# Pinned magnitudes, a norm moved by one attention pair, score banks for the gated layer, and shifted blocks in one fused fp32 kernel

## The chip, the cores and the metric

One Trainium2 chip, and one core of it: the program uses no other. The metric is the device time of one execution in microseconds (us); lower is better. Five engines work beside each other and meet through semaphores: TensorE (PE, with its weight loads as PEld), VectorE (DVE), ScalarE (ACT), GpSimd (POOL) and SyncE (SP), whose queue issues every DMA transfer here.

## The reference

Attention with sigmoid in place of softmax, a gated layer with a root-mean-square norm, and a layer with a product of two projections. Weights come as float64 and are decoded on the chip.

```python
scores = scale * np.matmul(q, k.transpose(0, 1, 3, 2)) - np.log(S)   # q, k, v: (4, 12, 448, 64)
attn = 1.0 / (1.0 + np.exp(-scores))
x = np.matmul(attn, v)                                  # then (1792, 768)
rms = np.sqrt(np.mean(x * x, axis=-1, keepdims=True) + 1e-06)
xn = x / rms * rms_g
g = xn @ w_gate                                         # 768 -> 1536
x = (g * sigmoid(g) * (xn @ w_val)) @ w_out             # 1536 -> 768
h = (x @ w1) * (x @ w2) @ w3                            # 768 -> 1024 -> 1024
out = h @ w_out                                         # 1024 -> 768
```

## The kernel before

The work is done per batch (four batches of 448 tokens). Every matrix operand is split into a high and a low part in fp32r, and each product is three matmuls (`mm3`, L293 to L295). The stages follow each other on PE in this order:

- attention pairs 0 to 11 (batches 0 and 1, two heads to a pair, `visit` L406, one pair to a visit); meanwhile DVE and POOL decode and split the eight tiles o0 to o7 of the second `w_out` (`decode_wo2`) and the first tiles of `w3`;
- the first products w3·w_out (`w3o_group`, L330, results copied out by ACT at L340);
- the first half of the gated layer for batches 0 and 1 (`a_group` L579, for m = 0 to 5; four units to an m, with a further w3·w_out product behind each four), each unit 18 matmuls into one PSUM bank, then a sigmoid (ACT L584) and products (DVE L585, L589);
- attention pairs 12 to 23 (batches 2 and 3), one visit at a time, set between the other half of the gated units and the first `b_group` units by a running sum of costs (L694 to L700);
- the rest of `b_group`; beside it `x_blocks` (L508) makes the right-hand operands of the next stage on DVE and ACT;
- batches 2 and 3 by Strassen-Winograd with seven products instead of eight: the gated layer (`winograd` L521), then `b_units(1)`, then the next layer c for both pairs of batches with `d_units` between and behind.

A weight tile is loaded as float64 (`wd`, L94, two buffers), decoded by `to_float` (L97): the absolute value on ACT (L104) or, for the first six tiles, on DVE (L106), then DVE L109, L110, L118, L121 into `wf`; then split by ACT L128 (or POOL L130) and POOL L131 into `ws` (four buffers). The magnitude `mag` has one buffer. `wo2` tiles (o0 to o7) go the same way with the magnitude on DVE. "Ahead" tiles (`add_ahead`, table `AHEAD_B1`) are `w1`/`w2` tiles decoded early and put into DRAM for the c layer.

`rms_norm` (L440) sums over partitions with one matmul (PE L442, reading `acc`, which POOL L436 adds up) into one of the three banks of `ps_m`, and that bank is read by ACT L446 and DVE L447; then DVE L448 to L453 make r, which `split_x` (`load_x` L466, `split2` L309 to L312) needs. PSUM has three `ps_m` banks, one for attention's output, and four (two tiles of two) for scores, L391 reading the latter with the sigmoid; the third score block uses `ps_m` and L389.

The order on each engine is not the written one: a scheduler of the framework places each instruction by estimated times, and engines run their lists strictly in that order. `tc.keep_in_program_order(i)` pins an instruction behind those written before it. The diff touches `to_float`, `split_to`, `accumulate`, `a_group`, and the main sequence (L646 to L711).

Of the kernel before, what the change touches and what calls it, by code (L numbers as in the profile page):

```python
# [8 lines left out]
F32 = mybir.dt.float32  # L9
F32R = mybir.dt.float32r  # L10
U32 = mybir.dt.uint32
AF = mybir.ActivationFunctionType
# [17 lines left out]
W3_FIRST = 3  # L30


AHEAD_B1 = (1, 1, 1, 1, 0, 0)
AHEAD_B2 = (2, 2, 2, 1, 1, 0)
WH = 3 * P

# [6 lines left out]
def fused_kernel(ctx: ExitStack, tc: tile.TileContext, qkv, wg, wv, wo, w1, w2, w3, wo2, gam, out):  # L43
# [38 lines left out]
    def psm():  # L82
        return ps_m.tile([P, 512], F32, tag="m", bufs=3, name="psm")
# [10 lines left out]
        nc.sync.dma_start(out=d, in_=src.bitcast(U32))  # L94
        return t

    def to_float(raw, w, scalar=True):  # L97

        lo, hi = raw[:, :w, 0], raw[:, :w, 1]
        mag = wp.tile([P, WT], F32, tag="mag", bufs=1, name="mag")[:, :w]  # L100
        f = wp.tile([P, WT], F32, tag="wf", bufs=2, name="wf")
        u = f[:, :w].bitcast(U32)
        if scalar:
            nc.scalar.activation(mag, hi.bitcast(F32), AF.Abs)  # L104
        else:
            nc.vector.tensor_scalar(  # L106
                out=mag.bitcast(U32), in0=hi, scalar1=0x7FFFFFFF, scalar2=None, op0=ALU.bitwise_and
            )
        nc.vector.tensor_scalar(out=mag, in0=mag, scalar1=HI_MIN, scalar2=HI_MAX, op0=ALU.max, op1=ALU.min)  # L109
        nc.vector.tensor_scalar(  # L110
            out=u,
            in0=mag.bitcast(U32),
            scalar1=3,
            scalar2=0x3FFFFFFF,
            op0=ALU.logical_shift_left,
            op1=ALU.bitwise_and,
        )
        nc.vector.scalar_tensor_tensor(  # L118
            out=u, in0=hi, scalar=0xC0000000, in1=u, op0=ALU.bitwise_and, op1=ALU.bitwise_or
        )  # L120
        nc.vector.scalar_tensor_tensor(  # L121
            out=u, in0=lo, scalar=29, in1=u, op0=ALU.logical_shift_right, op1=ALU.bitwise_or
        )
        return f
# [8 lines left out]
    class Weights:  # L133
# [58 lines left out]
        def split_to(self, n):  # L192

            n = min(n, len(self.seq) - 1)
            while self.n_split <= n and len(self.split) < self.BUFS:
                i = self.n_split
                self.load_to(i)
                src, kt, double, keep, use = self.seq[i]
                f = self.raw.pop(i)
                w = WT if kt is None else kt * P  # L200
                if double:
                    f = to_float(f, w, i >= 2 * W3_FIRST)
                    if keep is not None:
                        nc.sync.dma_start(out=keep, in_=f[:, :w].rearrange("p (k c) -> p k c", c=P))
                    self.out -= 1
                self.finish()
                if not use:
                    self.n_split += 1
                    continue
                t = wp.tile([P, 2, WT], F32R, tag="ws", bufs=self.BUFS, name="ws")  # L210
                self.split[i] = [t, 2]
                self.n_split += 1
                if kt is None:
                    for j in range(2):
                        split_weight(t[:, :, j * WH : (j + 1) * WH], next(self.blocks), WH)
                elif double:
                    self.late = (i, t, f, w, i >= 2 * W3_FIRST)
                else:
                    split_weight(t, f, w)
                    self.out -= 1  # L220
# [73 lines left out]
        nc.tensor.matmul(ps, wh, xt[:, 1, :], start=False, stop=False)  # L294
        nc.tensor.matmul(ps, wh, xt[:, 0, :], start=False, stop=last)  # L295

    def accumulate(tiles, xts):
        ps = psm()[:, :S]
        n = len(xts)
        j = 0  # L300
        for t, kt in tiles:
            for kw in range(kt):
                mm3(ps, t, kw, xts[j], j == 0, j == n - 1)
                j += 1
        return ps
# [134 lines left out]
    def rms_norm(b):  # L440
        ps = psm()[:, :S]
        nc.tensor.matmul(ps, ones, acc.pop(b), start=True, stop=True)  # L442
        v = scratch("v")
        r = rms[b] = scr.tile([P, S], F32, tag="r", bufs=2, name="r")
        t = scratch("t")
        nc.scalar.activation(t, ps, AF.Sqrt, bias=eps_b, scale=1.0 / DM)  # L446
        nc.vector.tensor_scalar(out=v, in0=ps, scalar1=1.0 / DM, scalar2=EPS, op0=ALU.mult, op1=ALU.add)  # L447
        nc.vector.reciprocal(r, t)  # L448

        nc.vector.tensor_tensor(out=t, in0=r, in1=r, op=ALU.mult)  # L450
        nc.vector.tensor_tensor(out=t, in0=t, in1=v, op=ALU.mult)
        nc.vector.tensor_scalar(out=t, in0=t, scalar1=-0.5, scalar2=1.5, op0=ALU.mult, op1=ALU.add)
        nc.vector.tensor_tensor(out=r, in0=r, in1=t, op=ALU.mult)  # L453
# [19 lines left out]
    def split_x(b, k):  # L473

        if k < KD:
            ready.append(load_x(b, k))
        if k:
            t = acts["x", b, k - 1] = x_tile("x", b)
            split2(t, ready.pop(0), b == 1)
# [28 lines left out]
    def x_blocks(k):  # L508
        right_blocks(k, load_x(2, k), load_x(3, k), load_x(2, k + 3), load_x(3, k + 3))
# [68 lines left out]

    def a_group(m, b, which):  # L579
        t = W.get(i_a[m][which])  # L580
        ps = accumulate([(t, 6)], [acts["x", b, k] for k in range(KD)])
        if which == 0:
            s = scratch("s")
            nc.scalar.activation(s, ps, AF.Sigmoid)  # L584
            nc.vector.tensor_tensor(out=s, in0=ps, in1=s, op=ALU.mult)  # L585
            half[m, b] = s
        else:
            s = half.pop((m, b))
            nc.vector.tensor_tensor(out=s, in0=ps, in1=s, op=ALU.mult)  # L589
            t = h_tile("hm", m)  # L590
            split2(t, s)
            acts["h", b, m] = t
# [53 lines left out]
    for i in range(NA + 1):  # L646
        visit(i, (0, NA, 2))
        with tc.issue_after(last_raw[0]):
            if i in DECODE:
                decode_wo2(DECODE[i])  # L650
                load_wo2(DECODE[i] + 2)
            if i in W3_AT:
                W.load_to(W3_AT[i] + 1)
                W.split_to(W3_AT[i] - 1)
        if i == HP:
            rms_norm(0)
        if i > HP:
            split_x(0, i - HP - 1)
    split_x(0, KD)


    def w3o_groups(kt):
        for nh in range(2):
            w3o_group(kt, nh)
            W.split_to(i_w3[kt][1] + 2 + nh)
            W.load_to(i_w3[kt][1] + 4 + nh)

    w3o_groups(0)
    rms_norm(1)
    for k in range(KD + 1):  # L670
        if k % 3 == 2:
# [22 lines left out]
    total, spent = sum(u[0] for u in beside), 0.0  # L694
    for j, u in enumerate(beside):
        spent += run(u, int(j >= half_a and j % 2 == 1))
        while visits and NP + 1 - NA - len(visits) < (NP + 1 - NA) * spent / total:
            visit(visits[0], (NA, NP, 1))
            if visits.pop(0) == NA + HP:
                rms_norm(2)  # L700
# [6 lines left out]
    pools["xw"] = pool("xw", "left")  # L707
    for j, u in enumerate(b[6:]):
        run(u, j % 2)
        if j % 2 == 0:  # L710
            x_blocks(j // 2)  # L711


    for m in range(KF1):
# [75 lines left out]
```

## Time and profile before

| | us |
|---|---|
| median of 3 runs | 1122.58 (1122.19 to 1125.78) |
| the profiled execution | 1121.57 |
| its span in the trace | 1119.8 |
| PE busy (share of span) | 1079.6 (96%) |
| DVE busy | 730.1 (65%) |
| ACT busy | 469.0 (42%) |
| POOL busy | 434.6 (39%) |
| mean granted clock of PE | 0.988 |

The span lacks 1.8 us of the execution, and the execution lies 1.0 us below the median. Times in rows count from the start of the span. A bracket at the end of a row, as [2.50 <-POOL acc L436], is the time its engine had nothing to do before it, and what ended that. PEclk is the share of full speed that PE was granted in a stretch: 1.0 is 2.4 GHz, 0.5 is 1.2 GHz.

### The profile page before, as it was taken

What the parts mean: (1) busy time and instruction counts of PE and PEld (TensorE: products, weight loads), DVE (VectorE), ACT (ScalarE), POOL (GpSimd) and SP (SyncE); (2) the same over time, 40 slices, a digit from 0 to 9 for tenths busy, and PEclk for the clock granted to TensorE, in tenths of its full rate; (3) what the DMA queues carried; (4) which work ended last, traced back from release to release, by engine and by line L of the source; (5) the groups of instructions that cost most, each with busy time, mean ns of one, the idle gap of its engine ahead of it and who ended that gap; (6) DMA issues with size and microseconds to landing.
All of it is one profiled execution on the core that took longest, in us unless ns stands there. A gap on an engine that the chain in (4) does not pass through costs nothing. (4 is left out here: it accounts for less than half of the span.)

```text
span 1119.8 us, 14158 instructions
## 1 busy us (share of the span) xinstructions
PE 1079.6 (96%) x5132; PEld 897.4 (80%) x5132; DVE 730.1 (65%) x996; ACT 469.0 (42%) x811; POOL 434.6 (39%) x336
## 2 busy tenths in 40 slices
PE   8996999998999999999999999999999999999998
PEld 3334988996766667699899999889989999999997
DVE  5985975567444645369889988666788726677500
ACT  5762433343455554534444443344433335333221
POOL 2743322333122113223566564223465533565420
PEclk9998999999999999999999999999999999999999
DMA  7733455447354355565111212676421243220131
GB/s 248 258 121 100 132 180 174 147 155 279 133 185 143 133 198 193 189 206 180 66 58 58 75 66 70 219 264 221 144 90 60 82 143 132 74 76 29 44 100 50
DMA packets 60981, 153.23 MB, mean 137 GB/s; under 512 B 5872, under 2 KB 32624, under 8 KB 60912
## 3 DMA queue, kind: packets, MB, share of 16 engines
q1 hardware_dynamic: 60912, 152.33, 40.0%
q8 instruction: 41, 0.67, 0.2%
q14 instruction: 28, 0.23, 0.1%
HBM read 114.95 MB, written 37.36 MB: 136 GB/s over the span
## 5 line engine op out<-in xcount | busy, mean ns | idle before, releaser
L131 POOL TENSOR_TENSOR ws<-wf,ws 128x768 fp32r<-128x768 f32 (+1 forms) x88 | 150.0, 1707 | 382.8 <-ACT ws L128 312.8
L293 PE MATMUL w<-w,ws 128*128 128x448 f32 x588 | 217.4, 370 | 4.4 <-POOL ws L131 2.2
L294 PE MATMUL w<-w,ws 128*128 128x448 f32 x588 | 217.4, 370 | 0.7 <-DVE w L312 0.7
L295 PE MATMUL w<-w,ws 128*128 128x448 f32 x588 | 216.7, 369 | 0.0
L131 POOL TENSOR_TENSOR ws<-wd,ws 128x384 fp32r<-128x384 f32 x112 | 128.4, 1161 | 92.1 <-ACT ws L128 85.3
L131 POOL TENSOR_TENSOR ws<-s,ws 128x384 fp32r<-128x384 f32 x84 | 99.0, 1183 | 79.2 <-ACT ws L128 77.4
L104 ACT ACTIVATE mag<-wd 128x768 f32<-128x768 f32 (+1 forms) x62 | 53.9, 869 | 178.7 <-DMA wd<-in_w 54.6
L293 PEld LDWEIGHTS w<-w,ws 128*128 128x128 f32 x588 | 111.1, 189 | 17.2 <-POOL ws L131 2.6
L294 PEld LDWEIGHTS w<-w,ws 128*128 128x128 f32 x588 | 111.2, 189 | 11.2 <-DVE w L312 1.0
L295 PEld LDWEIGHTS w<-w,ws 128*128 128x128 f32 x588 | 111.3, 189 | 10.6
L293 PE MATMUL psm<-x,ws 128*128 128x448 f32 x288 | 108.7, 377 | 8.0 <-DVE s L585 5.3
L110 DVE TENSOR_SCALAR wf<-mag 128x768 uint32<-128x768 uint32 (+1 forms) x76 | 57.1, 752 | 84.8 <-POOL ws L131 78.0
L293 PE MATMUL psm<-hm,ws 128*128 128x448 f32 x288 | 106.8, 371 | 1.1 <-POOL ws L131 1.1
L294 PE MATMUL psm<-hm,ws 128*128 128x448 f32 x288 | 105.8, 367 | 0.5 <-DVE hm L312 0.5
L294 PE MATMUL psm<-x,ws 128*128 128x448 f32 x288 | 106.1, 369 | 0.0
L295 PE MATMUL psm<-x,ws 128*128 128x448 f32 x288 | 106.1, 368 | 0.0
L295 PE MATMUL psm<-hm,ws 128*128 128x448 f32 x288 | 105.3, 365 | 0.0
L109 DVE TENSOR_SCALAR mag<-mag 128x768 f32<-128x768 f32 (+1 forms) x76 | 49.8, 655 | 51.4 <-ACT mag L104 50.9
L128 ACT ACTIVATE ws<-wf 128x768 fp32r<-128x768 f32 (+1 forms) x82 | 61.3, 750 | 51.2 <-PE psm L295 22.7
L118 DVE SCALAR_TENSOR_TENSOR wf<-wd,wf 128x768 uint32<-128x768 uint32 (+1 forms) x76 | 80.9, 1064 | 2.2
L128 ACT ACTIVATE ws<-wd 128x384 fp32r<-128x384 f32 x112 | 54.5, 514 | 58.3 <-PE w L295 34.5
L121 DVE SCALAR_TENSOR_TENSOR wf<-wd,wf 128x768 uint32<-128x768 uint32 (+1 forms) x76 | 77.3, 1016 | 1.5
(113 smaller groups left out, 1991.7 us busy)
## 6 DMA issues: line engine op xcount, KB each, us to landing
raw<-in_qkv SPq DMA_DIRECT2D x23, 736.0 KB, 4.5
wd<-in_wo SPq DMA_DIRECT2D x20, 768.0 KB, 5.8
wd<-in_w SPq DMA_DIRECT2D x16, 768.0 KB, 5.2
wd<-w SPq DMA_DIRECT2D x32, 384.0 KB, 3.6
wd<-in_wg SPq DMA_DIRECT2D x12, 768.0 KB, 4.7
wd<-in_wv SPq DMA_DIRECT2D x12, 768.0 KB, 4.6
wd<-in_w SPq DMA_DIRECT2D x16, 512.0 KB, 4.4
w<-wf SPq DMA_DIRECT2D x16, 384.0 KB, 2.5
```

The lines of the kernel that those rows point to most:

```text
L104: nc.scalar.activation(mag, hi.bitcast(F32), AF.Abs)
L109: nc.vector.tensor_scalar(out=mag, in0=mag, scalar1=HI_MIN, scalar2=HI_MAX, op0=ALU.max, op1=ALU.min)
L110: nc.vector.tensor_scalar(out=u, in0=mag.bitcast(U32), scalar1=3, scalar2=0x3FFFFFFF, op0=ALU.logical_shift_left, op1=ALU.bitwise_and,)
L118: nc.vector.scalar_tensor_tensor(out=u, in0=hi, scalar=0xC0000000, in1=u, op0=ALU.bitwise_and, op1=ALU.bitwise_or)
L121: nc.vector.scalar_tensor_tensor(out=u, in0=lo, scalar=29, in1=u, op0=ALU.logical_shift_right, op1=ALU.bitwise_or)
L128: nc.scalar.activation(t[:, 0, :w], f[:, :w], AF.Copy)
L131: nc.gpsimd.tensor_tensor(out=t[:, 1, :w], in0=f[:, :w], in1=t[:, 0, :w], op=ALU.subtract)
L293: nc.tensor.matmul(ps, wl, xt[:, 0, :], start=first, stop=False)
L294: nc.tensor.matmul(ps, wh, xt[:, 1, :], start=False, stop=False)
L295: nc.tensor.matmul(ps, wh, xt[:, 0, :], start=False, stop=last)
```

## The change

Seven edits. In the new file the lines are two higher from L106 on (L442 is L444, L312 is L314), and more behind L580 (L585 is L591).

1. The magnitudes of weight tiles 6 to 9 (the first four of the gated layer) are pinned in program order.
2. The first norm comes after visit 7 instead of visit 6, the six `split_x(0, ...)` follow one visit later; the last one is written behind the first w3·w_out product.
3. `a_group` for batch 1 and m < 6 takes its PSUM bank from the score tiles (`psa`).
4. The running sum that places the second attention's visits is measured from 8.0, so the first visit comes after three units instead of one.
5. `x_blocks` are written at units 0, 1, 2 of `b[6:]` instead of 0, 2, 4.
6. `AHEAD_B1` is all ones: two more tiles are decoded ahead beside `b_units(0)`.
7. With it, two fewer are decoded beside the c layer (they were in front of its second group).

```diff
-AHEAD_B1 = (1, 1, 1, 1, 0, 0)
+AHEAD_B1 = (1, 1, 1, 1, 1, 1)
...
-    def to_float(raw, w, scalar=True):
+    def to_float(raw, w, scalar=True, pin=False):
...
-            nc.scalar.activation(mag, hi.bitcast(F32), AF.Abs)
+            i = nc.scalar.activation(mag, hi.bitcast(F32), AF.Abs)
+            if pin:
+                tc.keep_in_program_order(i)
...
-                    f = to_float(f, w, i >= 2 * W3_FIRST)
+                    f = to_float(f, w, i >= 2 * W3_FIRST, i < 2 * W3_FIRST + 4)
...
-    def accumulate(tiles, xts):
-        ps = psm()[:, :S]
+    def accumulate(tiles, xts, ps=None):
+        ps = psm()[:, :S] if ps is None else ps
...
-        ps = accumulate([(t, 6)], [acts["x", b, k] for k in range(KD)])
+        ps = None
+        if b and m < KF1 // 2:
+
+            ps = ps_sc.tile([P, 2, 512], F32, tag="sc", bufs=2, name="psa")[:, 0, :S]
+        ps = accumulate([(t, 6)], [acts["x", b, k] for k in range(KD)], ps)
...
-        if i == HP:
+        if i == HP + 1:
             rms_norm(0)
-        if i > HP:
-            split_x(0, i - HP - 1)
-    split_x(0, KD)
+        if i > HP + 1:
+            split_x(0, i - HP - 2)
...
+    split_x(0, KD - 1)
     w3o_groups(0)
+    split_x(0, KD)
     rms_norm(1)
...
-        while visits and NP + 1 - NA - len(visits) < (NP + 1 - NA) * spent / total:
+        while visits and NP + 1 - NA - len(visits) < (NP + 1 - NA) * (spent - 8.0) / (total - 8.0):
...
-        if j % 2 == 0:
-            x_blocks(j // 2)
+        if j < 3:
+            x_blocks(j)
```

**The first norm on DVE.** Before, around DVE's reading of the norm's bank (`v<-psm`); the 128x768 rows are the decoding of o7, the 128x512 ones of `w3` tiles:

```order
L106 TENSOR_SCALAR mag<-wd 128x768
L109 TENSOR_SCALAR mag<-mag 128x768
L447 TENSOR_SCALAR v<-psm 128x448
L448 RECIPROCAL r<-t 128x448
L110 TENSOR_SCALAR wf<-mag 128x768
L450 TENSOR_TENSOR t<-r 128x448
L118 SCALAR_TENSOR_TENSOR wf<-wd,wf 128x768
```

Now:

```order
L111 TENSOR_SCALAR mag<-mag 128x768
L112 TENSOR_SCALAR wf<-mag 128x768
L120 SCALAR_TENSOR_TENSOR wf<-wd,wf 128x768
L108 TENSOR_SCALAR mag<-wd 128x512
L123 SCALAR_TENSOR_TENSOR wf<-wd,wf 128x768
L111 TENSOR_SCALAR mag<-mag 128x512
...
L112 TENSOR_SCALAR wf<-mag 128x512
L120 SCALAR_TENSOR_TENSOR wf<-wd,wf 128x512
L123 SCALAR_TENSOR_TENSOR wf<-wd,wf 128x512
L449 TENSOR_SCALAR v<-psm 128x448
L450 RECIPROCAL r<-t 128x448
```

The reading of the bank came behind the second step of o7's decoding. It now comes behind the rest of that decoding and two whole `w3` tiles (13 instructions after o7's second step).

**The end of the first attention on ACT.** Before, the last two visits (`xr<-av` begins the work of a visit):

```order
L424 ACTIVATE xr<-av 128x448
L435 ACTIVATE sq<-xr 128x448
L391 ACTIVATE a<-sc,bias_s 128x896
L104 ACTIVATE mag<-wd 128x768
L391 ACTIVATE a<-sc,bias_s 128x896
L389 ACTIVATE a<-psm,bias_s 128x448 x2
L424 ACTIVATE xr<-av 128x448
L435 ACTIVATE sq<-xr 128x448
L340 ACTIVATE w3ot<-psm 128x384
L104 ACTIVATE mag<-wd 128x768
```

Now:

```order
L426 ACTIVATE xr<-av 128x448
L437 ACTIVATE sq<-xr 128x448
L393 ACTIVATE a<-sc,bias_s 128x896 x2
L391 ACTIVATE a<-psm,bias_s 128x448 x2
L426 ACTIVATE xr<-av 128x448
L437 ACTIVATE sq<-xr 128x448
L342 ACTIVATE w3ot<-psm 128x384 x2
...
L342 ACTIVATE w3ot<-psm 128x384
L311 ACTIVATE x<-xs 128x448
L342 ACTIVATE w3ot<-psm 128x384
L104 ACTIVATE mag<-wd 128x768
```

The magnitude of tile 6 stood between the two score sigmoids of the last scored pair; it now stands behind the fourth w3·w_out copy.

**The way into the Winograd stage on DVE.** L163 to L165 before (L165 to L167 now) make the first sums of a Winograd weight, which product 1 needs; w1 is its right-hand operand for the last third. Before, the first of these blocks stood in front of all three `x_blocks`:

```order
L450 TENSOR_TENSOR t_3644<-r_3643 128x448
L163 TENSOR_TENSOR s_4018<-wd_3881 128x384
L451 TENSOR_TENSOR t_3644<-t_3644,v_3642 128x448
L164 TENSOR_TENSOR s_4018<-s_4018,wd_3881 128x384
L452 TENSOR_SCALAR t_3644<-t_3644 128x448
L165 TENSOR_TENSOR wd_3881<-wd_3881 128x384
L453 TENSOR_TENSOR r_3643<-r_3643,t_3644 128x448
L466 SCALAR_TENSOR_TENSOR xs_3726<-xs_3726,g_sb_86,r_2843 128x448
```

Now, at the end of the third `x_blocks`:

```order
L112 TENSOR_SCALAR wf_4065<-mag_4064 128x768
L506 TENSOR_TENSOR xs_3926<-xs_3926,t1_3932 128x448
L314 TENSOR_TENSOR w1_3944<-t1_3932,w1_3944 128x448
L314 TENSOR_TENSOR w3_3948<-xs_3923,w3_3948 128x448
L314 TENSOR_TENSOR w4_3952<-xs_3926,w4_3952 128x448
L120 SCALAR_TENSOR_TENSOR wf_4065<-wd_4008,wf_4065 128x768
L165 TENSOR_TENSOR s_4117<-wd_4072 128x384
L123 SCALAR_TENSOR_TENSOR wf_4065<-wd_4008,wf_4065 128x768
L166 TENSOR_TENSOR s_4117<-s_4117,wd_4072 128x384
L167 TENSOR_TENSOR wd_4072<-wd_4072 128x384
```

The first weight sums now come behind the last `x_blocks`, with the decoding of one of the two extra ahead tiles (wf_4065) between.

## Rows read from the trace of the kernel before

**Rows 1.** The page, part 1: busy time of each engine.

```profile
PE 1079.6 (96%) x5132; PEld 897.4 (80%) x5132; DVE 730.1 (65%) x996; ACT 469.0 (42%) x811; POOL 434.6 (39%) x336
```

**Rows 2.** Timeline of PE, first norm: start, us, engine, line, operation [idle before].

```profile
48.62 0.92 PE L386 MATMUL psm<-raw 64*128 64x448 f32 x4
52.03 1.40 PE L442 MATMUL psm<-acc,ones 128*128 128x448 f32 x2 [2.50 <-POOL acc L436]
...
60.19 0.92 PE L386 MATMUL psm<-raw 64*128 64x448 f32 x4
...
66.76 0.92 PE L386 MATMUL psm<-raw 64*128 64x448 f32 x4
```

**Rows 3.** Timeline of PE, single idle times that the sum uses.

```profile
99.67 3.25 PE L404 MATMUL av<-a,raw 128*64 128x448 f32 x8 [10.46 <-ACT a L391]
...
278.54 1.86 PE L374 MATMUL psm<-raw 128*128 128x448 f32 x2 [2.85 <-DVE s L585]
...
539.11 0.67 PE L293 MATMUL w<-w,ws 128*128 128x448 f32 x2 [1.48 <-ACT w L309]
...
816.04 0.47 PE L293 MATMUL w<-w,ws 128*128 128x448 f32 x1 [2.24 <-POOL ws L131]
```

**Rows 4.** Waits of PE: who waited for whom, us in total, times, longest.

```profile
PE psm L293 <- DVE s L585: 5.3, 3, 2.4
```

**Rows 5.** Windows: busy time (instructions) of each engine, then PEclk, DMA share, GB/s.

```profile
100.00:105.00 5.00, 5.00 (x18) 2.79 (x15) 0.00 (x0) 1.79 (x4) 0.64 (x1) 0.63 0.01 5
130.60:270.00 139.40, 133.86 (x686) 124.95 (x687) 94.39 (x136) 53.70 (x88) 39.50 (x23) 1.00 0.57 190
280.00:284.00 4.00, 4.00 (x12) 3.37 (x11) 0.56 (x1) 1.96 (x3) 0.00 (x0) 0.50 0.86 296
505.50:541.80 36.30, 34.16 (x164) 30.52 (x163) 32.77 (x49) 18.14 (x36) 14.73 (x9) 0.98 0.47 156
540.00:544.00 4.00, 3.34 (x9) 2.81 (x9) 3.33 (x7) 1.51 (x3) 1.34 (x2) 0.58 0.00 0
```

**Rows 6.** Timeline of ACT, last scored pair of the first attention.

```profile
97.83 0.89 ACT L104 ACTIVATE mag<-wd 128x768 f32<-128x768 f32 x1 [10.75 <-DMA wd<-in_wg]
```

**Rows 7.** Timeline of DVE around the first norm, and a `w3` tile.

```profile
49.02 1.97 DVE L110 TENSOR_SCALAR wf<-mag 128x768 uint32<-128x768 uint32 x1
...
55.28 0.61 DVE L447 TENSOR_SCALAR v<-psm 128x448 f32<-128x448 f32 x1
...
58.67 0.49 DVE L110 TENSOR_SCALAR wf<-mag 128x768 uint32<-128x768 uint32 x1
...
61.02 0.94 DVE L121 SCALAR_TENSOR_TENSOR wf<-wd,wf 128x768 uint32<-128x768 uint32 x1
...
94.37 0.43 DVE L110 TENSOR_SCALAR wf<-mag 128x512 uint32<-128x512 uint32 x1
94.83 0.69 DVE L118 SCALAR_TENSOR_TENSOR wf<-wd,wf 128x512 uint32<-128x512 uint32 x1
```

**Rows 8.** Timeline of POOL, a split of the first attention.

```profile
48.58 2.00 POOL L131 TENSOR_TENSOR o<-wf,o 128x768 fp32r<-128x768 f32 x1
```

**Rows 9.** Timeline of ACT, the change back from the norm's function.

```profile
54.13 1.28 ACT L375 ACT_TABLE_LOAD   x1
55.42 0.63 ACT L375 ACTIVATE al<-psm,bias_s 128x448 f32<-128x448 f32 x1
```

**Rows 10.** Timeline of DVE, `x_blocks`: first row, last row and the one behind.

```profile
505.47 1.27 DVE L466 SCALAR_TENSOR_TENSOR xs<-xs,g_sb,r 128x448 f32<-128x448 f32 x2
...
540.72 1.15 DVE L312 TENSOR_TENSOR w<-xs,w 128x448 fp32r<-128x448 f32 x2
541.79 0.55 DVE L164 TENSOR_TENSOR s<-s,wd 128x384 f32<-128x384 f32 x1
```

**Rows 11.** The page, part 5: splits of 384 columns, mean ns before the last bar.

```profile
L131 POOL TENSOR_TENSOR ws<-s,ws 128x384 fp32r<-128x384 f32 x84 | 99.0, 1183 | 79.2 <-ACT ws L128 77.4
L128 ACT ACTIVATE ws<-wd 128x384 fp32r<-128x384 f32 x112 | 54.5, 514 | 58.3 <-PE w L295 34.5
```

## The prediction

> **What bounds the kernel now.** I read the page first: PE is busy 1079.6 us, 96% of the span [rows 1], so what can be gained is PE's idle time and what the clock takes after it. Second, the timeline of PE with its brackets, where the idle times stand singly: the reader is to see that few and large ones make most of the loss, and that each has a named releaser [rows 2, 3]; three of one kind are grouped in the view of waits [rows 4]. Third, the windows, for the clock: where PE stood, it is granted half of its full speed for some us afterwards [rows 5]. The losses, in order of place:
> - The first norm stretches its visit: 48.62 to 60.19 is 11.57 us, the next visit, 60.19 to 66.76, 6.57 [rows 2]. That is 5.0 lost, 2.50 of it waiting for POOL's sum.
> - The largest: 10.46 at 99.67 [rows 3]. From 100 to 105 the clock averages 0.63, so half speed held for 0.74 of it, to 103.7; 4.0 us of work at half speed cost 2.0 more. Sum 12.5.
> - 5.3 for a bank that DVE L585 frees, three times in the gated layer [rows 4].
> - 2.85 at 278.54 in the second attention; the window 280 to 284 is all at 0.50 [rows 3, 5], so from 278.54 to 284 at least 2.7 is lost too. Sum 5.6.
> - 1.48 at 539.11, 0.66 idle in the window 540 to 544, clock 0.58 there [rows 3, 5]: some 1.5 from the clock. Sum 3.6.
> - 2.24 at 816.04 [rows 3], and by the pattern of 540 to 544 some 1.7 from the clock. Sum 3.9.
>
> **The change part by part.** *The pin.* ACT stood 10.75 us for the load of tile 6 [rows 6] with the second score sigmoid behind it; PE's 10.46 is that sigmoid's lateness. In the new order the magnitude stands behind the fourth w3·w_out copy, with the load issued as early as before, as the buffer of tile 4 comes free. Behind it on ACT stand the copies that free PE's banks; before the fourth copy lie 96 matmuls of that stage, some 18 us at 133.86 / 686 = 0.195 each [rows 5], which is longer than the wait was. So the sigmoids go at once: **+12.5**. Bounds: 12.5, and 8 if the first gated tile, now split just as its stage begins, is several us late.
>
> *The norm, one pair later.* POOL's sum has by then been done for a visit, so the 2.50 goes. What is late next is DVE. Its reading of the norm's bank stands behind 13 more instructions, and PE wants that bank again for the second half of the third score block of visit 8: 48.62 + 2 x 6.57 + 0.7 for the norm's matmul (half of its 1.40, which ran at the lower clock) + 0.4 is about 62.8. DVE comes to the first of the 13 at 55.3, where the reading stood before [rows 7]. Without any disturbance they take 0.49 + 2 x 0.94 for the rest of o7 and 6 x 0.43 + 4 x 0.69 for two `w3` tiles, 7.7, and the reading 0.61: 63.6, a wait of 0.8. But an L110 took 1.97 beside POOL's subtraction of 2.00 and 0.49 without one [rows 7, 8]: it was held for 1.5. Four such subtractions fall into the stretch, two of 768 columns and two of 512; at 1.5 and 1.0 each they add 5: 68.6, a wait of 5.8. I take 5.8, since DVE and POOL work in just this pattern there; 0.8 and 7.2 (POOL's conversions hold it too) stay as ends. With 0.7 for the matmul and 1.8 from the clock the place costs 8.3 against 5.0: **-3.3**. Between no bank wait (0.7 in place of 5.0) and 7.2 plus 3 (if the attention outputs, whose eight buffers DVE frees after the norm, are late as well): +4.3 to -7.7.
>
> The Trainium skill (GPSIMD Engine Reference, Key points) says that GpSimd shares its SBUF interfaces with VectorE, and that they contend where DVE has two SBUF inputs or runs in a mode of two ports. By that rule the steps with two inputs, L120 and L123, are held as L112 is, and the -3.3 stands; were only the one-input steps of my row held, the wait would be nearer 3 and the part -0.5.
>
> ACT changes its function for the norm and back. The row has 1.28 for a load, and the next activation starts 1.29 after it [rows 9]; both loads fit beside the bank wait. By the Trainium skill (ScalarE: Activation LUTs, What ACT_TABLE_LOAD costs) a switch is 2.66 us with a drain; this trace does not show the drain. By that figure the sigmoid behind would be 2.8 later, nothing while the bank wait covers it, 2.8 where there is none.
>
> *Lent score banks.* Units of batch 1 no longer need one of the three banks that DVE frees late; the score tiles are idle then. What is late next is the weights: four tiles to an m of 23.2 us, DVE busy 94.39 of 139.40 [rows 5], 15.7 for an m. That leaves room: **+5.3**, down to 0 if each wait becomes one on weights.
>
> *The second attention, later by two units.* The wait at 278.54 came from DVE's product standing in line with the decoding of tiles whose loads compete with the pairs' own (DMA share 0.86 [rows 5]). The visits are now spread closer (the same number over the same units less 8.0 of cost) but the queue of gated tiles is further on at the first. Magnitudes still stand between sigmoids there. I take half of the 5.6: **+2.8**, between +5.6 and -3.
>
> *x_blocks and the ahead tiles beside b.* The three blocks run on DVE back to back from the norm's r to 541.87, 36.4 us, with DVE busy 32.77 of 36.30 [rows 5, 10]. Writing them earlier can take out only the 3.5 it stood idle: they end near 538.3. But now a tile's decoding and the first weight sums come behind them: 0.49 + 2 x 0.94 and 2 x 0.55, then an ACT copy of 0.51 and a subtraction of 1.18 [rows 7, 10, 11], of which 0.49 lies ahead; together 4.7 to 5.2, so 543. PE arrives at product 1 at 539.11 - 1.48 = 537.6. A wait of 5.4 and 1.8 from the clock is 7.2 against 3.6: **-3.6**. Ends: +3.6 (DVE three blocks early by as much as the written order) and -6.
>
> *The ahead tiles that leave the c layer* take the chain in front of 816.04 away; 0.4 is left: **+3.5**, between +3.9 and 0. The two extra decodings beside b are under PE there (DVE is the engine with the work, and its price is in the part before).
>
> Sum: 12.5 - 3.3 + 5.3 + 2.8 - 3.6 + 3.5 = 17.2. The profiled execution goes from 1121.57 to 1104.4; the median stands 1.0 above, so I forecast **1105.4**.
>
> **The rivals.** *One or both new waits do not come* (0.25). The scheduler's lists hold only the order: should DVE reach the bank in time, the norm is worth +4.3 in place of -3.3, and 1097.8; should the third block end by 533, x_blocks are worth +3.6 in place of -3.6, and 1098.2; both, 1090.6 (0.08 of the 0.25). For: the undisturbed sum is only 0.8 late. Against: L110 at 1.97.
>
> *The gain is given back in small waits* (0.20). Banks lent, but PE then waits for weights; the attention shift yields nothing; the first gated tile is late by 4: 5.3 + 2.8 of the sum gone makes 1113.5, with the tile 1117. For: before, every stage has a tile chain ACT, DVE, ACT, POOL with one magnitude buffer. Against: DVE's 68% in that stage.
>
> *The pin only moves the wait* (0.03). If the load of tile 6 came later than the fourth copy, ACT would hold the copies and PE the next product: 12.5 back, 1117.9. For: ACT's order is strict. Against: 18 us of room.
>
> *Slower: the tile chain paces the gated layer* (0.04). With tiles 6 to 9 begun later, if a tile's way took over a quarter of an m from then on, PE would wait every m. It is slower once this costs 17.2 + 3.4 = 20.6 over six m, 3.4 each: four tiles in 26 us instead of 22.3. That is 1126 and more. Against: 15.7 of DVE in 23.2.
>
> **How the numbers follow.** The forecast has 0.48. The range 1095 to 1116 takes in the forecast's own ends (1100 to 1111 with the terms that are most in doubt, the bank wait and the x_blocks), one clean wait, and most of the given-back case; it leaves out both clean (0.08), the moved pin, the slower case and a tail of the second rival, 0.18. A change of 0.3%, 3.4 us, is about what a measurement of this kernel can tell. Faster by more: forecast, first rival, nearly all of the second, most of the third: 0.91; within: 0.05; slower: 0.04.
>
> **What would show it.** Right: PE has no 10 us idle near 90 and starts the w3·w_out products about 9 us earlier (12.5 less 3.3); a wait of 4 to 7 on DVE's reading (L449) near 62; no wait on L591 in the first gated half; a wait of some 5 on POOL's split at product 1 of the first Winograd m; no idle at the second group of c. Wrong: no bank wait near 62 (then nearer 1098), PE waiting for ws in the gated layer again and again (then 1113 or more).

## The result, and the profile after

The changed kernel takes 1111.17 us (median of 4 runs, 1108.64 to 1111.74) against 1122.38 for the kernel before (4 runs, 1118.96 to 1125.78); the ratio is 0.9896, 95% interval 0.9862 to 0.9930. It is faster, by 1.0%, and 5.8 above the forecast of 1105.4, inside its range. The profiled execution took 1108.64 with a span of 1106.5, 13.3 less than before. It is the fastest of its four, 2.5 below their median: the traces show 13.3 of a change of which the medians show 11.2.

The page, part 1, answers to [rows 1]: PE has less to wait for and the same work.

```profile
PE 1077.3 (97%) x5132; PEld 896.1 (81%) x5132; DVE 735.2 (66%) x996; ACT 469.6 (42%) x811; POOL 439.8 (40%) x336
```

Where the 13.3 us came from is read from the timeline of PE, by the start of the first matmul of each stage. All numbers are in us. The lead is before minus after; "added" is how much of it the stretch in front of that matmul gave, and "forecast" holds the terms of the sum that fall into that stretch.

| first matmul of | before | after | lead | added | forecast |
|---|---|---|---|---|---|
| w3·w_out products | 102.86 | 94.56 | 8.30 | +8.3 | +9.2 |
| gated layer | 130.63 | 122.74 | 7.89 | -0.4 | 0 |
| m = 5 | 252.56 | 238.49 | 14.07 | +6.2 | +5.3 |
| Winograd, gated | 534.38 | 524.08 | 10.30 | -3.8 | +2.8 |
| b, batches 2 and 3 | 694.75 | 686.14 | 8.61 | -1.7 | -3.6 |
| c, first pair | 785.82 | 776.48 | 9.34 | +0.7 | 0 |
| d, first pair | 893.58 | 880.32 | 13.26 | +3.9 | +3.5 |

Behind d nothing differs. One row is far off: "Winograd, gated", the stretch that holds the second attention.

**The end of the first attention.** Timeline of ACT, answering to [rows 6]: the two score sigmoids go together, the 10.75 us for a tile's load are gone.

```profile
89.95 1.89 ACT L393 ACTIVATE a<-sc,bias_s 128x896 f32<-128x896 f32 x2
91.73 1.16 ACT L391 ACTIVATE a<-psm,bias_s 128x448 f32<-128x448 f32 x2
```

**The norm.** Timeline of PE, answering to [rows 2]:

```profile
55.02 0.92 PE L388 MATMUL psm<-raw 64*128 64x448 f32 x4
55.87 1.02 PE L444 MATMUL psm<-acc,ones 128*128 128x448 f32 x2
57.08 1.02 PE L376 MATMUL psm<-raw 128*128 128x448 f32 x2 [0.19 <-ACT a L391]
...
67.99 1.85 PE L388 MATMUL psm<-raw 64*128 64x448 f32 x2 [4.29 <-DVE v L449]
...
77.24 0.92 PE L388 MATMUL psm<-raw 64*128 64x448 f32 x4
```

Timeline of DVE in the queue in front of that reading:

```profile
55.27 1.98 DVE L112 TENSOR_SCALAR wf<-mag 128x768 uint32<-128x768 uint32 x1
...
60.79 2.18 DVE L120 SCALAR_TENSOR_TENSOR wf<-wd,wf 128x512 uint32<-128x512 uint32 x1
...
65.04 1.63 DVE L120 SCALAR_TENSOR_TENSOR wf<-wd,wf 128x512 uint32<-128x512 uint32 x1
...
67.32 0.62 DVE L449 TENSOR_SCALAR v<-psm 128x448 f32<-128x448 f32 x1
```

Timeline of POOL, its subtractions there; the fourth begins behind the reading:

```profile
54.84 2.01 POOL L133 TENSOR_TENSOR o<-wf,o 128x768 fp32r<-128x768 f32 x1
...
60.55 1.87 POOL L133 TENSOR_TENSOR o<-wf,o 128x768 fp32r<-128x768 f32 x1
...
64.81 1.32 POOL L133 TENSOR_TENSOR ws<-wf,ws 128x512 fp32r<-128x512 f32 x1
...
68.16 1.26 POOL L133 TENSOR_TENSOR ws<-wf,ws 128x512 fp32r<-128x512 f32 x1
```

The reader sees the forecast wait (4.29 for 5.8), and what stretched the queue: an L120 of 512 columns took 2.18 and 1.63 where POOL subtracts, 0.69 alone [rows 7]. Windows of all engines, PEclk third from the end:

```profile
68.00:72.00 4.00, 4.00 (x5) 1.66 (x6) 3.93 (x3) 0.96 (x2) 2.42 (x3) 0.50 0.00 0
72.00:76.00 4.00, 4.00 (x16) 1.16 (x16) 3.04 (x6) 0.53 (x2) 0.56 (x1) 0.82 0.00 0
```

At half speed from 67.99 to about 73.4 (0.82 in 72 to 76 is half for 0.36 of 4 us), PE lost another 2.7. The whole is read from the starts of the visits: from 55.02 to 77.24 it is 22.2 for two visits, which take 13.1 where nothing waits (6.56 each from 35.33 to 55.02). The norm's place costs 9.1, against 5.0 before.

**The second attention.** Timeline of PE in its first visit, answering to 278.54 in [rows 3]:

```profile
264.35 1.77 PE L388 MATMUL sc<-raw 64*128 64x448 f32 x8
267.78 1.02 PE L388 MATMUL psm<-raw 64*128 64x448 f32 x2 [1.66 <-DVE s L591]
269.19 1.02 PE L388 MATMUL psm<-raw 64*128 64x448 f32 x2 [0.39 <-DVE s L595]
272.61 1.86 PE L376 MATMUL psm<-raw 128*128 128x448 f32 x2 [2.41 <-DVE s L591]
277.47 0.74 PE L295 MATMUL psm<-x,ws 128*128 128x448 f32 x1 [3.00 <-ACT a L391]
```

Timeline of ACT there:

```profile
270.01 0.89 ACT L104 ACTIVATE mag<-wd 128x768 f32<-128x768 f32 x1 [5.10 <-DMA wd<-in_wg]
...
271.27 0.53 ACT L590 ACTIVATE s<-psm 128x448 f32<-128x448 f32 x1
...
272.42 1.00 ACT L393 ACTIVATE a<-sc,bias_s 128x896 f32<-128x896 f32 x1
275.04 0.97 ACT L104 ACTIVATE mag<-wd 128x768 f32<-128x768 f32 x1 [1.61 <-DVE wf L112]
275.92 0.98 ACT L393 ACTIVATE a<-sc,bias_s 128x896 f32<-128x896 f32 x1
276.81 1.12 ACT L391 ACTIVATE a<-psm,bias_s 128x448 f32<-128x448 f32 x2
```

Timeline of DVE:

```profile
271.94 0.61 DVE L591 TENSOR_TENSOR s<-psm,s 128x448 f32<-128x448 f32 x1
274.45 0.56 DVE L112 TENSOR_SCALAR wf<-mag 128x768 uint32<-128x768 uint32 x1 [1.89 <-POOL ws L133]
```

In the kernel before, the other wait of that visit beside the 2.85 was

```profile
274.68 1.02 PE L386 MATMUL psm<-raw 64*128 64x448 f32 x2 [1.15 <-DVE s L589]
```

Idle times of 7.5 (1.66 + 0.39 + 2.41 + 3.00) stand where before there were 4.0 (1.15 + 2.85). The 2.41 is the fault that the pin took out of the first attention: a magnitude waits 5.10 us for its load, with the sigmoid L590 behind it on ACT and DVE's L591, which frees PE's bank, behind that. The 3.00 has a second magnitude between the two score sigmoids, but that one waits for DVE's L112, which waits for POOL's split, and not for a load. The first two stand behind DVE's decoding of the tile before.

**The way into Winograd.** Timeline of PE, answering to 539.11 in [rows 3]:

```profile
530.41 0.47 PE L295 MATMUL w<-w,ws 128*128 128x448 f32 x1 [4.30 <-POOL ws L133]
```

The forecast had 5.4 on POOL's split at this product.

### The profile page after: what moved, and what is told of

It is laid out like the page before. It is cut to its first block, busy times and chain, and to the rows that moved or that the text cites. A ratio compares the mean times of both kernels' runs of the same rounds, so it can differ in the third digit from the quotient of the medians.

```text
span 1106.5 us, 14161 instructions
## 1 busy us (share of the span) xinstructions
PE 1077.3 (97%) x5132; PEld 896.1 (81%) x5132; DVE 735.2 (66%) x996; ACT 469.6 (42%) x811; POOL 439.8 (40%) x336
## 5 line engine op out<-in xcount | busy, mean ns | idle before, releaser
L133 POOL TENSOR_TENSOR ws<-wf,ws 128x768 fp32r<-128x768 f32 (+1 forms) x88 | 153.7, 1748 | 356.6 <-ACT ws L130 299.7
L133 POOL TENSOR_TENSOR ws<-wd,ws 128x384 fp32r<-128x384 f32 x112 | 132.0, 1192 | 83.4 <-ACT ws L130 76.3
L296 PEld LDWEIGHTS w<-w,ws 128*128 128x128 f32 x588 | 110.8, 188 | 10.2
L112 DVE TENSOR_SCALAR wf<-mag 128x768 uint32<-128x768 uint32 (+1 forms) x76 | 57.6, 758 | 67.5 <-POOL ws L133 64.9
L295 PE MATMUL psm<-x,ws 128*128 128x448 f32 x216 | 81.2, 376 | 6.0 <-ACT a L391 3.4
L120 DVE SCALAR_TENSOR_TENSOR wf<-wd,wf 128x768 uint32<-128x768 uint32 (+1 forms) x76 | 84.7, 1115 | 2.2
L123 DVE SCALAR_TENSOR_TENSOR wf<-wd,wf 128x768 uint32<-128x768 uint32 (+1 forms) x76 | 79.5, 1047 | 1.4
L296 PE MATMUL psm<-x,ws 128*128 128x448 f32 x216 | 79.8, 369 | 0.0
L297 PE MATMUL psm<-x,ws 128*128 128x448 f32 x216 | 79.6, 368 | 0.0
```

The costliest lines, as they stand in the source:

```text
L112: nc.vector.tensor_scalar(out=u, in0=mag.bitcast(U32), scalar1=3, scalar2=0x3FFFFFFF, op0=ALU.logical_shift_left, op1=ALU.bitwise_and,)
L120: nc.vector.scalar_tensor_tensor(out=u, in0=hi, scalar=0xC0000000, in1=u, op0=ALU.bitwise_and, op1=ALU.bitwise_or)
L123: nc.vector.scalar_tensor_tensor(out=u, in0=lo, scalar=29, in1=u, op0=ALU.logical_shift_right, op1=ALU.bitwise_or)
L133: nc.gpsimd.tensor_tensor(out=t[:, 1, :w], in0=f[:, :w], in1=t[:, 0, :w], op=ALU.subtract)
L295: nc.tensor.matmul(ps, wl, xt[:, 0, :], start=first, stop=False)
```

## The experiments

Starts of stages are from each run's timeline of PE. Ratios are to the kernel before, run beside it on the same chip.

**u_pin: edit 1 undone.**

```diff
-                    f = to_float(f, w, i >= 2 * W3_FIRST, i < 2 * W3_FIRST + 4)
+                    f = to_float(f, w, i >= 2 * W3_FIRST, False)
```

> The changed kernel with edit 1 undone: no magnitude is pinned. ACT's list again has the magnitude of tile 6 between the two score sigmoids of the last scored pair. Theory: PE stands for 8 to 11 us for that sigmoid near 87 and runs at the lower clock for 3 to 4 us after it; the w3 products start 10 to 13 us later than 94.56, and the time rises by 9 to 13 us, to 0.998 to 1.001 of before. Rival (the pin only moves the wait, and a later stage has it): the time rises by less than 4.

Ratio 1.0021 (1.0004 to 1.0038). Timeline of ACT:

```profile
89.86 0.99 ACT L393 ACTIVATE a<-sc,bias_s 128x896 f32<-128x896 f32 x1
99.76 0.90 ACT L104 ACTIVATE mag<-wd 128x768 f32<-128x768 f32 x1 [8.90 <-DMA wd<-in_wg]
100.56 0.99 ACT L393 ACTIVATE a<-sc,bias_s 128x896 f32<-128x896 f32 x1
```

Timeline of PE:

```profile
101.60 3.25 PE L406 MATMUL av<-a,raw 128*64 128x448 f32 x8 [8.56 <-ACT a L393]
```

The w3 products start at 104.78, 10.2 later than with the pin. Without it the whole change gains nothing: the ratio lies just above the expected 0.998 to 1.001. The pin is worth 10.2 at this place and not 12.5 (12.8 at the last matmul). PE comes there 3.8 later than in the kernel before, made later by the norm, and the load only 1.9 later (ACT has it at 99.76 for 97.83), so that PE has 1.9 less to wait (8.56 for 10.46). Pin and norm do not simply add.

**u_norm: edit 2 undone.**

```diff
-        if i == HP + 1:
+        if i == HP:
             rms_norm(0)
-        if i > HP + 1:
-            split_x(0, i - HP - 2)
+        if i > HP:
+            split_x(0, i - HP - 1)
+    split_x(0, KD)
...
-    split_x(0, KD - 1)
     w3o_groups(0)
-    split_x(0, KD)
```

> The changed kernel with edit 2 undone: the first norm after visit 6 again, DVE reading its bank behind two steps of o7's decoding. Theory: the wait for DVE L449 (4.29 us at 67.99) goes and the wait for POOL's sum (2.5 near 52) is back; the norm's place costs 5.0 instead of about 7, the w3 products start 1 to 3 us earlier than 94.56, and the time is 1 to 3 us lower than the changed kernel's. Rival (the norm is better late, the wait for DVE is covered anyway): the start of the w3 products at 94.5 or later, the time not lower.

Ratio 0.9889 (0.9859 to 0.9919). The w3 products start at 88.55, 6.0 earlier; the theory holds, more strongly than expected. Of the 6.0, 1.5 are missing in best3, where the order is the same up to there: behind POOL's sum the clock stayed full in this execution and fell in that one (last section). At the start of the gated layer 4.9 of it is left (117.85), at the end of the last matmul 1.75 (1101.29 against 1103.04). The move of the norm is a loss where it stands; what it costs at the end of this kernel is less than the timing of the two can tell (best3 below asks again).

**n_pin: the DVE magnitudes of the w3 tiles pinned too.**

```diff
-            nc.vector.tensor_scalar(
+            i = nc.vector.tensor_scalar(
                 out=mag.bitcast(U32), in0=hi, scalar1=0x7FFFFFFF, scalar2=None, op0=ALU.bitwise_and
             )
+            if pin:
+                tc.keep_in_program_order(i)
```

> The changed kernel with the DVE magnitudes of the w3 tiles pinned in program order too (two lines). On DVE the norm's reading of its bank then stands behind o7 and one w3 tile instead of two. Theory (the wait at 67.99 is DVE's queue, stretched by POOL): the reading starts near 64 instead of 67.3, PE's wait falls from 4.29 to 1 to 2, the w3 products start 3 to 5 us earlier than 94.56 (a shorter wait brings less of the lower clock), and the time falls by 1 to 4, part of the lead being given back at the waits for weights behind. Rival (the reading waits for something else, such as the ACT table or the sum): the wait stays at 4 or more.

Ratio 0.9912 (0.9896 to 0.9928). The wait for the norm's bank all but goes (the four matmuls of that block take 2.04 in all, with no idle time the view shows), and the w3 products start at 88.96, 5.6 earlier: DVE's queue was the cause. But the time is not lower. Timeline of PE (lines behind L110 are two higher in this run):

```profile
115.47 0.69 PE L340 MATMUL psm<-o,ws 128*128 128x384 f32 x1 [4.65 <-POOL ws L135]
```

The last of the six `w3` tiles is decoded from 108.39 on, behind the second norm, where the changed kernel decodes it from 95.56 on in front of it, and is late for its product. A miss in the time: at the start of the gated layer 1.5 of the lead is left (121.28), at m = 5 0.3.

**u_psa: edit 3 undone.**

```diff
-        if b and m < KF1 // 2:
+        if False:
```

> The changed kernel with edit 3 undone: units of batch 1 use the three banks again. Theory: three waits for DVE L591 (1.2 to 2.4 each) return in the first gated half, which lengthens by 5 to 6.5 us (from its first matmul at 122.74 to unit m = 6 at 253.14, 130.4 us in the changed kernel), while the second attention's loss stays within 2 us of the changed kernel's. The time rises by 4 to 6, to 0.993 to 0.995 of before. Rival (PE being early causes the loss at the second attention): the waits return, but the idle time at the first visit falls by 4 or more, and the time stays within 1.5 us.

Ratio 0.9941 (0.9923 to 0.9959). Two waits for DVE return, 3.21 and 1.42, of the three expected. The longer, timeline of PE:

```profile
185.69 0.47 PE L295 MATMUL psm<-x,ws 128*128 128x448 f32 x1 [3.21 <-DVE s L591]
```

m = 5 starts 8.5 later (247.03), and from there to the Winograd stage it takes 282.3 against 285.6: 3.3 comes back. The idle time at the first visit is 6.0 (0.54, 1.97, 3.50) for 7.5. So a part of the loss at the second attention goes with PE being early: the rival has a share, though not most of it. The 8.5 is no sure price of the banks: the execution traced here lies 3.0 above this run's median, and by the ratios (0.9941 for 0.9896) undoing them costs 5.0, near the forecast of 5.3.

**u_shift: edit 4 undone.**

```diff
-        while visits and NP + 1 - NA - len(visits) < (NP + 1 - NA) * (spent - 8.0) / (total - 8.0):
+        while visits and NP + 1 - NA - len(visits) < (NP + 1 - NA) * spent / total:
```

> The changed kernel with edit 4 undone: the second attention's visits are placed by spent / total again, so the first visit comes after one unit of m = 6 instead of three. Theory: the shift itself made the way into the second attention dearer, because the first visit now meets a magnitude between its two score sigmoids and two more in front of them (ACT), each waiting for its tile's load. Then the idle time of PE around the first visit (9.9 us of brackets over 100 ns in the changed kernel, between 265 and 278) falls to 4 to 5, as in the kernel before, and the time falls by 3 to 6 us against the changed kernel, to 0.983 to 0.987 of before. Rival: the loss comes from PE being early (banks lent, no waits in the gated layer), so that the tiles' loads are late whatever the placing; then the idle time at the first visit stays at 8 to 11 and the ratio at 0.989.

Ratio 0.9910 (0.9887 to 0.9934), which does not differ from the changed kernel's. From m = 5 to Winograd it takes 281.4, 4.2 less; at the last matmul 2.3 is left (1100.76). But a wait stays, timelines of PE and DVE:

```profile
264.76 1.86 PE L388 MATMUL sc<-raw 64*128 64x448 f32 x4 [5.41 <-DVE s L595]
```

```profile
260.48 0.56 DVE L111 TENSOR_SCALAR mag<-mag 128x768 f32<-128x768 f32 x1 [2.24 <-ACT mag L104]
...
264.10 0.61 DVE L595 TENSOR_TENSOR s<-psa,s 128x448 f32<-128x448 f32 x1
```

The idle time at the first visit is 7.2 (with 1.32 and 0.51 beside the 5.41), not the 4 to 5 that the theory expected, and the time missed its range. Each theory had part: the shift itself cost 4.2, and without it the first visit still stands for 5.4 behind DVE, which waits for the same magnitudes. The bank that it stands for is a score bank that edit 3 lent (`psa`): the last unit of m = 5 still had it.

**late: the decoding written behind the visits, and eight tiles pinned**, on u_shift.

```diff
-        spent += run(u, int(j >= half_a and j % 2 == 1))
+        more = int(j >= half_a and j % 2 == 1)
+        W.load_to(u[2] + 2 + more)
+        u[1]()
+        spent += u[0]
...
+        W.split_to(u[2] + 1 + more)
+        W.load_to(u[2] + 3 + more)
```

(with `or 28 <= i < 36` in the condition of the pin)

> The changed kernel with edit 4 undone (as u_shift) and, in the loop of the second attention, each unit's decoding of later tiles written behind the visit that follows the unit, with the magnitudes of tiles 28 to 35 pinned. On ACT the sigmoids of the first visit then stand ahead of the magnitudes that wait for loads. Theory (the way into the second attention is dear because magnitudes, each waiting for its load, stand before the work that frees PE's banks, on ACT and through it on DVE): idle time around the first visit falls from 7 in u_shift to under 2, from the start of unit m = 5 to the Winograd stage (281.4 in u_shift) 5 to 9 less, and the time falls by 3 to 8 against u_shift. Rival (the tiles then come late for PE's units instead): waits for POOL L133 of 2 us and more appear between 270 and 330 and eat the gain.

Ratio 1.0062 (1.0042 to 1.0081): the rival. The first visit has no wait over 0.4, but PE waits for POOL's splits; in total, times, longest:

```profile
PE psm L295 <- POOL ws L133: 14.1, 6, 3.4
```

and m = 5 to Winograd takes 302.9. Four units behind a visit, at 269.14, 295.80, 326.95 and 354.59, find their tiles not split (10.8 of the 14.1). **best2**, the edits of n_pin, u_xb and late in one kernel:

> The three edits of n_pin, u_xb and late in one kernel. If each is worth what its theory says where it stands, the w3 products start 3 to 5 earlier, the second attention costs 9 to 12 less than in the changed kernel, the Winograd stage is entered 2 to 4 earlier: 12 to 18 less than the changed kernel in the trace, and a ratio to before of 0.973 to 0.981. Rival (PE being early is given back at weight waits): 0.982 or more, with new waits for POOL L133.

Ratio 1.0106 (1.0090 to 1.0123), with the same waits; the rival again.

**p30_31: one magnitude pinned**, that of tile 30, on u_shift.

```diff
-                    f = to_float(f, w, i >= 2 * W3_FIRST, i < 2 * W3_FIRST + 4)
+                    f = to_float(f, w, i >= 2 * W3_FIRST, i < 2 * W3_FIRST + 4 or 30 <= i < 31)
```

> The changed kernel with edit 4 undone (as u_shift) and the magnitude of tile 30 alone pinned as well, nothing else deferred. On ACT the sigmoids of the first visit of the second attention then stand ahead of the magnitudes of tiles 30 and 31, and the later tiles float as before. Theory (two magnitudes that wait for their loads hold the first visit; in the run named late it was the deferral and the pins of the later tiles that made tiles late): the idle time around the first visit falls from about 7 in u_shift to under 2, from unit m = 5 to the Winograd stage 5 to 9 less than the 281.4 of u_shift, no waits for POOL L133 over 2 us between 265 and 400, and the time falls to 0.982 to 0.986 of before. Rival (any delay of those tiles makes PE wait for weights): a wait for POOL L133 of 2 us or more behind the first visit, and the time like u_shift's or higher, 0.990 or more.

Ratio 0.9821 (0.9794 to 0.9849). Timeline of ACT in the first visit:

```profile
257.60 0.55 ACT L590 ACTIVATE s<-psm 128x448 f32<-128x448 f32 x1 [2.53 <-PE psm L297]
258.50 1.91 ACT L393 ACTIVATE a<-sc,bias_s 128x896 f32<-128x896 f32 x2 [0.36 <-PE sc L388]
260.30 1.16 ACT L391 ACTIVATE a<-psm,bias_s 128x448 f32<-128x448 f32 x2
...
266.21 0.89 ACT L104 ACTIVATE mag<-wd 128x768 f32<-128x768 f32 x1
268.38 0.93 ACT L104 ACTIVATE mag<-wd 128x768 f32<-128x768 f32 x1 [1.28 <-DVE wf L112]
```

The magnitudes stand behind the sigmoids and no longer wait for a load; PE has no wait over 0.2 in that visit, and m = 5 to Winograd takes 276.3, 5.1 less than u_shift and 9.3 less than the changed kernel. One pinned instruction shows the cause of what u_shift left: the two magnitudes in front of the sigmoids. With edit 4 in place the pin was not tried.

**u_xb: edit 5 undone.**

```diff
-        if j < 3:
-            x_blocks(j)
+        if j % 2 == 0:
+            x_blocks(j // 2)
```

> The changed kernel with edit 5 undone: x_blocks at units 0, 2, 4 again, the table of ahead tiles still all ones. The first weight sums of the Winograd stage then stand behind the first x_blocks instead of the last. Theory (the order on DVE made the wait for POOL's split): the wait of 4.3 at product 1 for POOL L133 goes, another of up to 2 for the last x_blocks takes its place as before; from the third norm to the second b stage (479.02 to 686.14, 207.1 us) 2 to 5 less; the time falls by 1.5 to 4. Rival (DVE's amount of work is what is late, wherever the sums stand): the idle time there stays at 4 or more, on the x_blocks.

Ratio 0.9934 (0.9913 to 0.9955): a miss. Timeline of PE:

```profile
532.20 1.11 PE L295 MATMUL w<-w,ws 128*128 128x448 f32 x2 [5.23 <-ACT w L311]
534.89 0.74 PE L296 MATMUL w<-w,ws 128*128 128x448 f32 x1 [0.83 <-DVE w L314]
```

The wait for POOL goes, and a longer one for the x_blocks comes; the third norm to the b stage takes 210.3 against 207.1 (the norm meant is `rms_norm(3)`, at 479.02, the last). With the extra ahead tiles in place, the earlier x_blocks are worth 3.2.

**u_ah: edits 6 and 7 undone.**

```diff
-AHEAD_B1 = (1, 1, 1, 1, 1, 1)
+AHEAD_B1 = (1, 1, 1, 1, 0, 0)
```

> The changed kernel with edits 6 and 7 undone: the table of ahead tiles as before, two of them decoded in front of the second group of c. Theory: the wait of 2.2 for POOL L131 at the second group of c returns with 1.5 to 1.7 from the clock, so the c stage (776.48 to 880.32, 103.84) takes 3.5 to 4.5 more; the first weight sums of the Winograd stage stand ahead of the x_blocks again, so from the third norm to the second b stage (207.12) it takes 1 to 4 less; together the time is the same to 3 higher. Rival (the extra tiles cost nothing beside b): the second stretch stays within 1 us, the time 3 to 5 higher.

Ratio 0.9915 (0.9887 to 0.9943). The third norm to the b stage takes 205.1, 2.0 less, and c 109.1, 5.3 more, with [rows 3]'s wait back:

```profile
809.01 0.72 PE L295 MATMUL w<-w,ws 128*128 128x448 f32 x1 [3.13 <-POOL ws L133]
```

The tiles cost 2.0 in front of Winograd, as expected, and save 5.3 in c, more than the 3.5 to 4.5 expected.

**best3: p30_31 with the norm after visit 6 (edit 2 undone).**

> p30_31 with the first norm after visit 6 again (edit 2 undone as in u_norm). Theory: what u_norm gave (1.75 us at the end in its trace, 6.0 at the start of the w3 products) and what p30_31 gives add up, less 1 to 3 that are given back at waits for weights: 1 to 2 us under p30_31, 0.980 to 0.985 of before. Rival (the lead of u_norm is used up at the second attention and the Winograd stage, where DVE is late whatever PE does): not lower than p30_31.

1096.74 us, ratio 0.9784 (0.9760 to 0.9808): it beats both kernels. The w3 products start at 90.04, Winograd at 510.14, and the last matmul ends 3.6 before that of p30_31 (1089.95 for 1093.50), more than the 1 to 2 expected. That later waits, once the second attention is mended, hide less of what the norm's move costs would explain it; no run here shows that by itself. **b4** places its six ahead tiles as 1, 1, 2, 2, 0, 0:

> best3 with the six ahead tiles beside the first b units placed as 1, 1, 2, 2, 0, 0 instead of one for each. None is then decoded in front of the Winograd stage, and on DVE the first weight sums stand ahead of the x_blocks again; the c layer keeps its lighter load. Theory (the wait of 3.6 for POOL's split at the first product 1 comes from an ahead tile and the weight sums standing behind the last x_blocks): that wait goes, 0.5 to 1.5 of waits for x_blocks take its place as in u_ah, from the third norm to the second b stage (206.7 in best3) 1 to 3 us less, c as in best3, and the time 1 to 3 lower than best3, 0.976 to 0.978 of before. Rival (the two tiles earlier hold DVE beside the last visits, or DVE reaches the x_blocks later by as much): the norm or the x_blocks come later, and the time is not lower than best3's.

1094.64 us, ratio 0.9781 (0.9759 to 0.9803): no different from best3. The wait in front of product 1 does fall; timelines of PE, best3 first:

```profile
515.76 0.47 PE L295 MATMUL w<-w,ws 128*128 128x448 f32 x1 [3.59 <-POOL ws L133]
```

```profile
515.73 0.47 PE L295 MATMUL w<-w,ws 128*128 128x448 f32 x1 [0.62 <-ACT w L311]
```

but smaller ones behind it and a gated layer that began 2.2 later (120.34 against 118.14) leave b4 only 1.0 ahead in the trace (last matmul ending at 1088.98 for 1089.95).

## Why the prediction was right, and where not

The sum was 17.2 and the trace gives 13.3; the medians lie 1.9 further off, by where the profiled execution fell among its runs. Most terms held in mechanism and nearly in size. One failed by 6.6, and the others together gave 2.6 more than forecast, so that the total fits partly by luck.

- *The pin, +12.5, and the norm, -3.3:* together 9.2, measured 8.3. The norm's place cost 9.1 for 8.3 forecast, by the starts of the visits. The wait was shorter than forecast (4.29 for 5.8), three of POOL's subtractions, not four, falling into DVE's queue, and the clock's part was longer (2.7 by PEclk for 1.8); 1.2 is the norm's own matmul and the 0.19 behind it (55.87 to 57.08), and 0.9 of the 9.1 is not parted further. So the move is -4.1; with 0.2 by which this execution was ahead in front of the norm (48.46 for 48.62), the pin's 12.5 came as 12.2. The two are not independent, as u_pin showed (10.2). Nor was the load of tile 6 "issued as early as before": it was issued at 95.67 for 93.49, and the gated layer begins with a wait of 2.15 for that tile's split.
- *Lent banks, +5.3:* 6.2 in the stage; 8.5 by undoing it in one trace, 1.6 of that at POOL's split (a wait of 2.08 at 128.94 for 0.48), and 5.0 by the ratios. The weights behind kept up: behind the first gated matmul there is no wait for POOL over 0.5 up to m = 5.
- *The second attention, +2.8: the step that failed.* "I take half of the 5.6" trusted the gated tiles to be further on at a first visit two units later. They were not: a tile's load was still out at 270.01. I had the magnitudes between the sigmoids before me ("Magnitudes still stand between sigmoids there") and did not price them: one held ACT for 5.10, of which 2.41 reached PE, and behind the other PE stood for 3.00. Measured: -3.8, with 7.5 of idle time and the clock behind it. The shift is 4.2 of it (u_shift), and 3.3 goes with PE's earliness (u_psa; these two were measured one at a time and overlap). p30_31, without the shift and with the magnitudes behind the sigmoids, has nothing of it left: m = 5 to Winograd takes 5.5 less than before, all of the 5.6 that I halved.
- *x_blocks, -3.6:* -1.7. The mechanism was right and the wait a little shorter (4.30 for 5.4). That this is the price of the extra tiles, with the earlier x_blocks a gain, was not separated; u_xb and u_ah did (+3.2 and -2.0).
- *c, +3.5:* 3.9; 5.3 by undoing it.
- *The rivals:* neither new wait stayed away, the tile chain did not pace the gated layer, and the pin did not move its wait. Of "given back in small waits" the gated layer shows little (2.15 for its first tile, where the rival had 4), but the shift that yields nothing did come; and n_pin and late show that waits for weights are close.

The changes of ACT's function cost what the rows said: the load of ACT's table behind the first norm took 1.28 again (59.52), it began 0.03 behind the activation before it, and the activation behind it began 1.29 later (60.81). The Trainium skill (ScalarE: Activation LUTs, What ACT_TABLE_LOAD costs) adds a drain to a switch; neither trace shows one. The Trainium skill says that GpSimd shares its SBUF interfaces with VectorE and that they contend where a VectorE instruction has two SBUF inputs (GPSIMD Engine Reference, Key points); the L120 of 2.18, which has two, agrees.

## What to carry to other kernels

Look in each engine's order for instructions that wait for a transfer and stand ahead of work that frees a bank or feeds the bound engine: they can cost up to the rest of the transfer (of ACT's 10.75 in the first attention 10.46 reached PE, of its 5.10 in the second 2.41; a wait of 7.59 on ACT at 421.60 of the changed kernel cost PE nothing that the trace shows). One pinned instruction was worth 7 us (last matmul of u_shift and p30_31, 1100.76 and 1093.50), while pinning eight of them with their loads deferred cost 21 in the same stage (302.9 and 281.4). Price a wait on a transfer as a point in time, not as a length: what makes the waiting engine later makes it shorter, unless it makes the transfer as much later. And an engine made earlier keeps its lead only as far as the next queue of weights reaches; undo one part at a time and read the lead stage by stage.

## What was not expected of the hardware

The clock does not answer to the length of one idle time alone. In u_norm PE stood for 1.91 in front of the gated layer and ran at half speed for a while; in the changed kernel it stood for 2.15 at the same place and stayed at full speed. Timeline of PE and a window of u_norm, then the same of the changed kernel:

```profile
117.85 0.47 PE L295 MATMUL psm<-x,ws 128*128 128x448 f32 x1 [1.91 <-POOL ws L133]
120.00:122.00 2.00, 2.00 (x7) 1.80 (x6) 1.88 (x4) 0.85 (x1) 0.49 (x1) 0.50 0.30 121
```

```profile
122.74 0.47 PE L295 MATMUL psm<-x,ws 128*128 128x448 f32 x1 [2.15 <-POOL ws L133]
122.00:126.00 4.00, 3.26 (x16) 3.04 (x17) 3.91 (x6) 1.78 (x3) 0.69 (x1) 1.00 0.32 108
```

Half speed also came after 2.24 at 816.04 in the kernel before and after 2.29 at the norm in best3 (0.64 in the window 816 to 820, 0.57 in 52 to 56 of best3), and not after 1.77 at the same norm in u_norm:

```profile
52.00:56.00 4.00, 4.00 (x16) 1.53 (x16) 3.93 (x6) 3.32 (x4) 2.47 (x2) 1.00 0.94 320
```

What decides it, these runs do not show. The price can be read: u_norm and best3 have the same order up to there, and the visit with the norm takes 9.2 in u_norm (48.94 to 58.10) and 11.3 in best3 (48.27 to 59.58). Of the 2.1 between them 0.5 is the wait, and the rest goes with the clock.
